# Decay attention in front of two MLPs: one group a bank for a chunk's output, and score products that alternate between heads

## The chip, the cores and the metric

The kernel runs on one core of one Trainium2 chip. The metric is the device time of one execution in microseconds (us), median of several runs.

## The reference

Decay attention over 2 batches, 8 heads, 768 tokens and 64 dimensions a head gives 1536 rows of 512. Two MLPs follow, the first gated, with 1536 hidden columns, the second with 2048:

```
intra = (q k^T * lam ** (i - j), i >= j) v
inter = (q * lam ** (i + 1)) state
state = lam ** block * state + (k * lam ** (block - 1 - j))^T v
x = intra + inter                        # all heads side by side: 1536 x 512
y = (silu(x @ w_gate) * (x @ w_val)) @ w_out
h = y @ w_in2 ;  out = (h * cos(h)) @ w_out2
```

The weights arrive as float64, all else is float32.

## The kernel before

The sequence is cut into chunks of 128 tokens: 12 chunks, six to a batch. Heads are taken in pairs; of a pair, one head's q and k, transposed, lie on partitions 0 to 63 and the other's on 64 to 127. A loop over g = 0 to 11 (here "turn g") issues, in this order and with no planner between:

- the score products of chunk g + 1 (L333: eight float32 products of 64 x 128 by 64 x 128, each run as two passes, first all four of one head of each pair into one PSUM bank, then all four of the other into a second bank), then two masking multiplications on VectorE (L338), which free the two banks;
- the transposes of q and k of chunk g + 2 (L276), copied out by ScalarE (L280, tiles qt and kt; VectorE makes qd at L284);
- in turns 6 to 11 one half of an MLP unit, twelve products (L96 to L98) on chunks that are already done;
- the state products (L309) with VectorE's addition (L320);
- the chunk's output, att_out: for each of the four pairs two score-value products (L350, 64 columns of weights, one for each half of the bank's partitions) and then, in all chunks but the first of a batch (10 of the 12), the state product of that pair (L355, 128 x 128), which adds to the same quarter of the bank. ScalarE and VectorE split the result (L90, L91: xh, xl).

Every engine takes its own instructions in that order. Loads are issued on SyncE (SP) in program order: q and k four chunks ahead, v three ahead, and in some turns one piece of weights (512 KB, tile raw, L123 and L128). The weights' float64 words are converted piecewise: `tick()` puts one VectorE step of a piece (L145, L149, L153, L158) behind a masking multiplication, a qd or a state addition. The first step of a piece also puts its absolute value on ScalarE (L143), and the last one the split (L90 on ScalarE, L91 on GpSimd). The first piece's steps stand in turn 3, where L143 comes ahead of the copies of chunk 5 on ScalarE, and L145 comes between the two maskings of chunk 4 on VectorE.

PSUM has four banks for transposes and scores (mm) and four for state, output and MLP sums (acc). Behind the attention the MLP units run with conversions between them.

Of the kernel before, what the change touches and what calls it, by code (L numbers as in the profile page):

```python
# [13 lines left out]
ALU = mybir.AluOpType  # L14
PSUM = bass.MemoryType.PSUM

# 2*pi = TWO_PI_1 + TWO_PI_2, TWO_PI_1 short so that n * TWO_PI_1 is exact in float32
TWO_PI_1 = 6.28125
TWO_PI_2 = 2.0 * math.pi - 6.28125

# [14 lines left out]
def kernel(  # L35
# [10 lines left out]
    w_out2: bass.AP,  # L46
    out: bass.AP,
):
    """Decay attention in chunks of 128 tokens, then the two MLPs with weights outermost:
    every tile of float64 weights is read once, turned into float32 on the chip and split  # L50
    there into two float32r parts of 12 significant bits each (w = wH + wL exactly); a
    product takes the passes wH xL + wL xH + wH xH."""
    nc = tc.nc
    B, H, S, D = q.shape
    P = 128
# [11 lines left out]
    CB = TB // C  # L67
    NBLK = NCH // CB

    # float64 words as pairs of int32 (low, high)  # L70
    w_gate, w_val, w_mid, w_in2, w_out2 = (w.bitcast(I32) for w in (w_gate, w_val, w_mid, w_in2, w_out2))

    const = ctx.enter_context(tc.tile_pool(name="const", bufs=1))
# [12 lines left out]
        return pool.tile([P, 512], F32, tag=where, name=where)  # L86

    def split(hi, lo, src, sub=None):
        """src = hi + lo exactly, each of 12 significant bits."""
        nc.scalar.activation(hi, src, AF.Copy)  # L90
        (sub or nc.vector).tensor_tensor(out=lo, in0=src, in1=hi.bitcast(F32), op=ALU.subtract)  # L91

    def mm3(ps, w, x, first, last):
        """ps += (wH + wL)^T (xH + xL), float32 products of 12-bit parts."""
        (wh, wl), (xh, xl) = w, x
        nc.tensor.matmul(ps, wh, xl, start=first, stop=False)  # L96
        nc.tensor.matmul(ps, wl, xh, start=False, stop=False)  # L97
        nc.tensor.matmul(ps, wh, xh, start=False, stop=last)  # L98

# [1 line left out]
    order1, order2 = [], []  # L101
    f0 = 0
    for n in GROUPS1:
# [25 lines left out]
        raw[key] = t  # L129

    def conv_steps():
        """float32 of the next piece: one vector instruction a step."""
        n = n_conv[0]
        n_conv[0] += 1
        key = pieces[n]
        words = raw.pop(key).rearrange("p (n t) -> p n t", t=2)
        lo, hi = words[:, :, 0], words[:, :, 1]
        w = cvt.tile([P, 512], I32, tag="cw", name="cw")
        t = cvt.tile([P, 512], F32, tag="ct", name="ct")
        pool = ring[n % (RING_A + RING_B) >= RING_A]  # L140
        wh = pool.tile([P, 512], F32R, tag="wh", name="wh")
        wl = pool.tile([P, 512], F32R, tag="wl", name="wl")
        nc.scalar.activation(t, hi.bitcast(F32), AF.Abs)  # L143
        # sign and top exponent bit, the low seven exponent bits and 23 of the mantissa
        nc.vector.tensor_scalar(  # L145
            out=w, in0=hi, scalar1=3, scalar2=0x3FFFFFF8, op0=ALU.logical_shift_left, op1=ALU.bitwise_and
        )
        yield
        nc.vector.scalar_tensor_tensor(  # L149
            out=w, in0=hi, scalar=-0x40000000, in1=w, op0=ALU.bitwise_and, op1=ALU.bitwise_or  # L150
        )
        yield
        nc.vector.scalar_tensor_tensor(  # L153
            out=w, in0=lo, scalar=29, in1=w, op0=ALU.logical_shift_right, op1=ALU.bitwise_or
        )
        yield
        # below float32's normal range the exponent bits left out are not the top bit's: zero there
        nc.vector.scalar_tensor_tensor(  # L158
            out=t, in0=t, scalar=2.0 ** -15, in1=w.bitcast(F32), op0=ALU.is_ge, op1=ALU.mult
        )  # L160
        split(wh, wl, t, sub=nc.gpsimd)
        wsp[key] = (wh, wl)
        yield
# [15 lines left out]
            pass  # L179
        load_piece()  # L180

# [1 line left out]
    att_stack = ExitStack()  # L183
    att = att_stack.enter_context(tc.tile_pool(name="att", bufs=2))
    qkv = {}
# [20 lines left out]
    state = [att.tile([P, NPAIR, P], F32, name=f"state{i}", bufs=1) for i in range(2)]  # L206

    def tables():
        """Powers of lam_h by doubling, falling (down[h, n] = lam_h ** (C - n), zero for n > C)
        and rising (up_p[h, n] = lam_h ** (n + 1)), and out to DRAM and back  # L210
        flip[j, h, C - 1 - i] = lam_h ** (i - j) where i >= j, else 0, and
        lrow[(h' d), pair, i] = lam_h ** (i + 1)."""
        flip = [att.tile([P, NPAIR, C], F32, tag="qd", name="qd", bufs=3) for _ in range(2)]
        anti = att.tile([P, P], F32, name="anti", bufs=1)
        nc.gpsimd.memset(anti, 0.0)
        nc.gpsimd.affine_select(
            out=anti, in_=anti, compare_op=ALU.not_equal, fill=1.0, base=1 - P, pattern=[[1, P]], channel_multiplier=1
        )
        nc.vector.memset(down[:, C + 1:], 0.0)
        nc.vector.memset(down[:, C:C + 1], 1.0)  # L220
        nc.sync.dma_start(down[:, C - 1:C], lam.rearrange("(h o) -> h o", o=1))
        n = 1
        while n < C:
            nc.vector.tensor_scalar(
                out=down[:, C - 2 * n:C - n], in0=down[:, C - n:C],
                scalar1=down[:, C - n:C - n + 1], scalar2=None, op0=ALU.mult,
            )
            n *= 2
        load_qkv(0, "qk")
        nc.sync.dma_start(down_d, down)  # L230
        nc.vector.tensor_copy(up_p[:, 0:1], down[:, C - 1:C])
        n = 1
        while n < C:
            nc.vector.tensor_scalar(
                out=up_p[:, n:2 * n], in0=up_p[:, 0:n], scalar1=up_p[:, n - 1:n], scalar2=None, op0=ALU.mult
            )
            n *= 2
        load_qkv(1, "q")
        e = down_d[:, :]
        for h2 in range(2):  # L240
            nc.sync.dma_start(
                flip[h2], bass.AP(e.tensor, e.offset + 1 + h2 * 2 * C, [[1, P], [4 * C, NPAIR], [1, C]])
            )
        nc.sync.dma_start(up_d, up_p)
        load_qkv(1, "k")
        load_qkv(0, "v")
        e = up_d[:, :]
        for h2 in range(2):
            nc.sync.dma_start(
                lrow[64 * h2:64 * h2 + 64], bass.AP(e.tensor, e.offset + h2 * C, [[0, 64], [2 * C, NPAIR], [1, C]])  # L250
            )
        return anti, flip

    def unflip(anti, flip):
        """dmask[j, h, i] = flip[i, h, C - 1 - j]: a head's flip is symmetric."""
        for h2 in range(2):
            ps = bank("acc")
            for p in range(NPAIR):
                nc.tensor.transpose(ps[:, p * C:(p + 1) * C], flip[h2][:, p, :], anti)
            nc.scalar.activation(dmask[:, h2::2, :], ps.rearrange("p (a i) -> p a i", a=NPAIR), AF.Copy)  # L260

# [1 line left out]
    xs = {}  # L263
    live = {}

# [31 lines left out]
            live[g, "kd"] = kd  # L297

    def att_state(g):
        """state(g + 1) = lam ** 128 * state(g) + k_dec^T v, block diagonal by head in a pair."""  # L300
        if g % CPB == CPB - 1:
            return
        kd, vn = live.pop((g, "kd")), qkv[g, "v"]
# [21 lines left out]
    def att_scores(g, before_mask=None, args=()):  # L325
        qt, kt = live[g, "qt"], live[g, "kt"]
        at = live[g, "at"] = att.tile([P, H, C], F32, tag="at", name="at")
        got = []
        for h2 in range(2):
            ps = bank("mm")  # L330
            r = slice(64 * h2, 64 * h2 + 64)
            for p in range(NPAIR):
                nc.tensor.matmul(ps[:, p * C:(p + 1) * C], kt[r, p, :], qt[r, p, :], start=True, stop=True)  # L333
            got.append(ps)
        if before_mask:
            before_mask(*args)
        for h2, ps in enumerate(got):
# [5 lines left out]
    def att_out(g):  # L343
        at, vn = live.pop((g, "at")), qkv[g, "v"]
        ps = bank("acc")
        inter = g % CPB != 0
        for p in range(NPAIR):
            cs = slice(p * C, (p + 1) * C)
            for h2 in range(2):
                nc.tensor.matmul(  # L350
                    ps[64 * h2:64 * h2 + 64, cs], vn[:, 2 * p + h2, :], at[:, 2 * p + h2, :],
                    start=True, stop=not inter,
                )
            if inter:
                nc.tensor.matmul(ps[:, cs], state[g % 2][:, p, :], live[g, "qd"][:, p, :], start=False, stop=True)  # L355
        xh, xl = x_tiles(g // CB)
        o = (g % CB) * C
        split(xh[:, :, o:o + C], xl[:, :, o:o + C], ps.rearrange("p (a i) -> p a i", a=NPAIR))

# [1 line left out]
    units = []  # L361
    for ph, order in enumerate((order1, order2)):
        for gi, fs in enumerate(order):
# [1 line left out]
                units += [(ph, gi, blk, f) for f in fs]  # L365
    NU = len(units)
    orders = (order1, order2)
    # the step that takes unit u's second product, and the steps a piece of weights is used in
    taken, t = [], 0
    for u in range(NU + LAG):  # L370
        while t < NU and t <= u - LAG:
# [31 lines left out]
        live[u] = (live[u], up_mm("val", f, x_tiles(blk), where))  # L403

    def produce(u):
        """The first product and the activation of unit u; what is left of it comes with finish()."""
        ph, gi, blk, f = units[u]
        if ph == 0:
            produce_gate(u)
            produce_val(u)  # L410
        else:
            up = up_mm("in2", f, x_tiles(blk, "y"))
            # cos(h) = sin(pi/2 - |h - 2 pi n|), n = round(h / 2 pi)
            n_ = tp.tile([P, TB], I32, tag="n", name="n")
            s = tp.tile([P, TB], F32, tag="s", name="s")
            nc.scalar.activation(n_, up, AF.Copy, scale=1.0 / (2.0 * math.pi))  # L416
# [55 lines left out]
                nc.sync.dma_start(out[r0:r0 + C, :], sm)  # L472

    def convert(u, due):
        """Convert what the units to come need, as slots come free and evenly over time."""
        while n_conv[0] < len(pieces):
            nxt = n_conv[0]
            if nxt >= RING and last_use[pieces[nxt - RING]] > u:
# [3 lines left out]
            conv_piece()  # L482
            due -= 1

# [1 line left out]
    with tc.manual_schedule():  # L486
        nc.vector.memset(halfpi, math.pi / 2)
        flip = tables()
# [96 lines left out]
```

## Time and profile before

| what | us |
| --- | --- |
| median of 3 runs | 646.48 (646.32 to 649.52) |
| span of the profiled execution, first to last instruction | 644.7 |
| TensorE (PE) busy in it | 631.7 (98%) |
| VectorE (DVE) busy | 455.3 (71%) |
| ScalarE (ACT) busy | 274.8 (43%) |

The page states no other time of the profiled execution than its span; the median of the runs is 1.8 us above it. Matmuls are pipelined and their ends are modelled, so TensorE's busy share says little: what a group of products occupies is read from its start to the start of the next group.

### The profile page before, as it was taken

The numbers are of one execution on the slowest core, as the hardware profiler recorded it, in microseconds if no ns is written. First come the engines' busy times: TensorE is split into PE (matmuls) and PEld (weight loads), VectorE is DVE, ScalarE is ACT, GpSimd is POOL, SyncE is SP. The second block draws the span as 40 slices with busy tenths as digits, with TensorE's granted clock in tenths as the row PEclk, the third lists the DMA queues.
The fourth block names the chain that finished last, engine by engine and source line by source line (L and its number), as shares of the span: only waits on it lengthen the run. The fifth ranks groups of instructions, "written<-read, shape, count | busy, mean of one in ns | idle before, by whom it ended". The sixth has DMA issues, their size and how long they took to land.

```text
span 644.7 us, 8244 instructions
## 1 busy us (share of the span) xinstructions
PE 631.7 (98%) x3176; PEld 517.4 (80%) x3176; DVE 455.3 (71%) x706; ACT 274.8 (43%) x464; POOL 131.3 (20%) x114
## 2 busy tenths in 40 slices
PE   6999999999999999999999999999999999999997
PEld 5778778888888878888888887788888888888885
DVE  4577746888889853388824478987797778776655
ACT  3333313555343421234313346555555555554441
POOL 1423312232332310023203244011101010100000
PEclk9999999999999999999999999999999999999999
DMA  7999312333343320034310111111111110000103
GB/s 170 219 213 225 108 34 66 104 126 111 118 131 106 127 63 1 32 99 130 99 34 15 52 57 41 35 64 37 62 41 58 36 63 2 0 1 0 67 3 128
DMA packets 66006, 49.56 MB, mean 77 GB/s; under 512 B 38816, under 2 KB 60848, under 8 KB 65968
## 3 DMA queue, kind: packets, MB, share of 16 engines
q1 hardware_dynamic: 65968, 49.04, 26.5%
q8 instruction: 25, 0.41, 0.3%
q14 instruction: 13, 0.11, 0.1%
HBM read 45.88 MB, written 3.16 MB: 76 GB/s over the span
## 4 chain that ended last, share of the span: by engine, by line
PE 73%; DVE 18%; ACT 6%; issue 1%; DMA 1%; DVEq 0%; SPq 0%; ACTq 0%
PE mm L97 11%; PE mm L96 11%; PE mm L98 11%; PE acc L96 10%; PE acc L98 10%; PE acc L97 10%; DVE cw L153 5%; DVE ct L158 3%; PE mm L333 3%; DVE cw L149 3%; PE acc L355 3%; PE acc L350 2%; PE mm L276 2%; DVE g L428 2%; DVE sum L466 2%; ACT wh L90 2%
## 5 line engine op out<-in xcount | busy, mean ns | idle before, releaser
L96 PE MATMUL mm<-xl,wh 128*128 128x512 f32 x456 | 177.5, 389 | 0.0
L97 PE MATMUL mm<-xh,wl 128*128 128x512 f32 x456 | 177.4, 389 | 0.0
L98 PE MATMUL mm<-xh,wh 128*128 128x512 f32 x456 | 177.4, 389 | 0.0
L91 POOL TENSOR_TENSOR wl<-ct,wh 128x512 fp32r<-128x512 f32 x68 | 91.4, 1345 | 390.2 <-ACT wh L90 390.2
L428 DVE TENSOR_TENSOR g<-s,mm 128x512 f32<-128x512 f32 x81 | 55.4, 683 | 65.5 <-PE mm L98 54.6
L98 PEld LDWEIGHTS mm<-xh,wh 128*128 128x128 f32 x456 | 85.6, 188 | 17.9
L96 PEld LDWEIGHTS mm<-xl,wh 128*128 128x128 f32 x456 | 85.6, 188 | 17.8
L97 PEld LDWEIGHTS mm<-xh,wl 128*128 128x128 f32 x456 | 85.6, 188 | 17.6
L90 ACT ACTIVATE wh<-ct 128x512 fp32r<-128x512 f32 x68 | 43.0, 633 | 122.9 <-DVE ct L158 122.9
L433 DVE TENSOR_TENSOR gl<-g,gh 128x512 fp32r<-128x512 f32 x84 | 58.5, 696 | 30.4 <-ACT gh L429 30.4
L96 PE MATMUL acc<-wl,gh 128*128 128x512 f32 x192 | 74.9, 390 | 1.5 <-DVE sum L464 1.1
L429 ACT ACTIVATE gh<-g 128x512 fp32r<-128x512 f32 x84 | 52.4, 624 | 53.3 <-DVE g L428 53.3
L98 PE MATMUL acc<-wh,gh 128*128 128x512 f32 x192 | 74.7, 389 | 0.0
L97 PE MATMUL acc<-wh,gl 128*128 128x512 f32 x192 | 74.7, 389 | 0.0
L153 DVE SCALAR_TENSOR_TENSOR cw<-raw,cw 128x512 int32<-128x512 int32 x68 | 67.5, 993 | 2.2
L419 ACT ACTIVATE s<-s 128x512 f32<-128x512 f32 x48 | 30.4, 633 | 72.8 <-DVE s L418 72.8
L96 PE MATMUL acc<-gl,wh 128*128 128x512 f32 x144 | 56.1, 390 | 1.5 <-DVE sum L466 1.5
L158 DVE SCALAR_TENSOR_TENSOR ct<-ct,cw 128x512 f32<-128x512 f32 x68 | 47.9, 705 | 11.7 <-ACT ct L143 6.2
L97 PE MATMUL acc<-gh,wl 128*128 128x512 f32 x144 | 56.0, 389 | 0.0
L98 PE MATMUL acc<-gh,wh 128*128 128x512 f32 x144 | 56.0, 389 | 0.0
L417 DVE SCALAR_TENSOR_TENSOR s<-n,mm 128x512 f32<-128x512 int32 x48 | 33.0, 687 | 30.7 <-ACT n L416 30.5
L149 DVE SCALAR_TENSOR_TENSOR cw<-raw,cw 128x512 int32<-128x512 int32 x68 | 49.3, 726 | 2.1
(67 smaller groups left out, 748.7 us busy)
## 6 DMA issues: line engine op xcount, KB each, us to landing
raw<-in_moe_w_out_dram SPq DMA_DIRECT2D x28, 512.0 KB, 3.2
raw<-in_moe_w_in_dram SPq DMA_DIRECT2D x16, 512.0 KB, 3.8
raw<-in_moe_w_gate_dram SPq DMA_DIRECT2D x12, 512.0 KB, 3.5
raw<-in_moe_w_val_dram SPq DMA_DIRECT2D x12, 512.0 KB, 3.6
q<-in_q_dram SPq DMA_DIRECT2D x12, 256.0 KB, 4.2
k<-in_k_dram SPq DMA_DIRECT2D x12, 256.0 KB, 4.4
v<-in_v_dram SPq DMA_DIRECT2D x12, 256.0 KB, 5.2
out_dram<-sum SPq DMA_DIRECT2D x12, 256.0 KB, 2.7
```

The lines of the kernel that those rows point to most:

```text
L90: nc.scalar.activation(hi, src, AF.Copy)
L91: (sub or nc.vector).tensor_tensor(out=lo, in0=src, in1=hi.bitcast(F32), op=ALU.subtract)
L96: nc.tensor.matmul(ps, wh, xl, start=first, stop=False)
L97: nc.tensor.matmul(ps, wl, xh, start=False, stop=False)
L98: nc.tensor.matmul(ps, wh, xh, start=False, stop=last)
L149: nc.vector.scalar_tensor_tensor(out=w, in0=hi, scalar=-0x40000000, in1=w, op0=ALU.bitwise_and, op1=ALU.bitwise_or)
L153: nc.vector.scalar_tensor_tensor(out=w, in0=lo, scalar=29, in1=w, op0=ALU.logical_shift_right, op1=ALU.bitwise_or)
L158: nc.vector.scalar_tensor_tensor(out=t, in0=t, scalar=2.0 ** -15, in1=w.bitcast(F32), op0=ALU.is_ge, op1=ALU.mult)
L417: nc.vector.scalar_tensor_tensor(out=s, in0=n_, scalar=-TWO_PI_1, in1=up, op0=ALU.mult, op1=ALU.add)
L428: nc.vector.tensor_tensor(out=g, in0=s, in1=up, op=ALU.mult)
L429: nc.scalar.activation(gh, g, AF.Copy)
L433: nc.vector.tensor_tensor(out=gl, in0=g, in1=gh.bitcast(F32), op=ALU.subtract)
```

## The change

In att_out all eight score-value products of a chunk come first and the four state products behind them. Only the first product in each half of the bank's partitions carries the start flag, and only the last one the stop flag, so the bank holds one accumulation group. In att_scores both banks are taken first, and the products go pair by pair, one head and then the other, each into its own bank. The rest of the diff strips comments and docstrings.

```
     def att_scores(g, before_mask=None, args=()):
         qt, kt = live[g, "qt"], live[g, "kt"]
         at = live[g, "at"] = att.tile([P, H, C], F32, tag="at", name="at")
-        got = []
-        for h2 in range(2):
-            ps = bank("mm")
-            r = slice(64 * h2, 64 * h2 + 64)
-            for p in range(NPAIR):
+        got = [bank("mm") for _ in range(2)]
+
+        for p in range(NPAIR):
+            for h2, ps in enumerate(got):
+                r = slice(64 * h2, 64 * h2 + 64)
                 nc.tensor.matmul(ps[:, p * C:(p + 1) * C], kt[r, p, :], qt[r, p, :], start=True, stop=True)
-            got.append(ps)
...
         inter = g % CPB != 0
+
         for p in range(NPAIR):
             cs = slice(p * C, (p + 1) * C)
             for h2 in range(2):
                 nc.tensor.matmul(
                     ps[64 * h2:64 * h2 + 64, cs], vn[:, 2 * p + h2, :], at[:, 2 * p + h2, :],
-                    start=True, stop=not inter,
+                    start=p == 0, stop=not inter and p == NPAIR - 1, skip_group_check=True,
                 )
-            if inter:
-                nc.tensor.matmul(ps[:, cs], state[g % 2][:, p, :], live[g, "qd"][:, p, :], start=False, stop=True)
+        if inter:
+            for p in range(NPAIR):
+                nc.tensor.matmul(
+                    ps[:, p * C:(p + 1) * C], state[g % 2][:, p, :], live[g, "qd"][:, p, :],
+                    start=False, stop=p == NPAIR - 1, skip_group_check=True,
+                )
```

## Rows read from the trace of the kernel before

**Rows 1.** The page: span, and busy time with shares and instructions.
```profile
span 644.7 us, 8244 instructions
...
PE 631.7 (98%) x3176; PEld 517.4 (80%) x3176; DVE 455.3 (71%) x706; ACT 274.8 (43%) x464; POOL 131.3 (20%) x114
```
**Rows 2.** Busy time by stretch, then clock, DMA share and GB/s.
```profile
20.00:27.00 7.00, 7.00 (x74) 5.42 (x71) 4.05 (x8) 1.68 (x3) 2.87 (x4) 1.00 1.07 209
27.00:33.20 6.20, 6.20 (x65) 4.74 (x65) 3.24 (x7) 1.68 (x3) 2.25 (x3) 1.00 1.15 246
...
67.50:76.60 9.10, 9.10 (x78) 6.97 (x77) 7.34 (x13) 3.88 (x7) 3.91 (x4) 1.00 0.08 27
```
**Rows 3.** Timeline of PE: start, us, line, operation, tiles, forms, count.
```profile
28.45 0.39 PE L350 MATMUL acc<-at,v 128*64 128x128 f32 x4
28.77 0.49 PE L355 MATMUL acc<-qd,state 128*128 128x128 f32 x2
29.18 0.44 PE L350 MATMUL acc<-at,v 128*64 128x128 f32 x4
...
31.55 1.71 PE L333 MATMUL mm<-qt,kt 64*128 64x128 f32 x16
33.19 0.66 PE L276 MATMUL mm<-ident,q 128*128 128x128 f32 x4
...
37.83 1.71 PE L333 MATMUL mm<-qt,kt 64*128 64x128 f32 x16
...
44.11 1.71 PE L333 MATMUL mm<-qt,kt 64*128 64x128 f32 x16
45.75 0.66 PE L276 MATMUL mm<-ident,q 128*128 128x128 f32 x4
```
**Rows 4.** Timeline of PE, turn 6, which has no state products of a chunk.
```profile
55.87 1.05 PE L350 MATMUL acc<-at,v 128*64 128x128 f32 x16
56.85 1.71 PE L333 MATMUL mm<-qt,kt 64*128 64x128 f32 x16
```
**Rows 5.** Waits from 12 to 98 us: who, for what, us, times, longest.
```profile
PEld acc L355 <- issue: 6.7, 39, 0.2
```
**Rows 6.** Score products (L333) under way in two instants: PE and PEld counts.
```profile
38.22:38.23 0.01, 0.01 (x2) 0.01 (x2) 1.00 1.19 256
38.72:38.73 0.01, 0.01 (x6) 0.01 (x3) 1.00 1.01 230
```
**Rows 7.** Timeline of ACT, turns 3 and 4.
```profile
35.47 0.68 ACT L143 ACTIVATE ct<-raw 128x512 f32<-128x512 f32 x1 [3.22 <-DMA raw<-in_moe_w_gate_dram]
...
36.53 0.59 ACT L280 ACTIVATE kt<-mm 128x512 f32<-128x512 f32 x1
...
41.33 0.60 ACT L280 ACTIVATE kt<-mm 128x512 f32<-128x512 f32 x1
```
**Rows 8.** Timeline of DVE, turns 3 and 4.
```profile
35.47 0.43 DVE L145 TENSOR_SCALAR cw<-raw 128x512 int32<-128x512 int32 x1 [1.90 <-DMA raw<-in_moe_w_gate_dram]
...
39.11 0.69 DVE L158 SCALAR_TENSOR_TENSOR ct<-ct,cw 128x512 f32<-128x512 f32 x1
40.98 0.69 DVE L91 TENSOR_TENSOR xl<-acc,xh 128x512 fp32r<-128x512 f32 x1 [1.18 <-ACT xh L90]
41.59 1.28 DVE L338 TENSOR_TENSOR at<-mm,dmask 128x512 f32<-128x512 f32 x2
```
**Rows 9.** Timeline of SP: the first piece of weights is issued.
```profile
28.98 1.06 SPq L123 DMA_DIRECT2D raw<-in_moe_w_gate_dram  x1
```
**Rows 10.** Timeline of PE: the first product behind the attention.
```profile
97.94 0.48 PE L96 MATMUL mm<-xl,wh 128*128 128x512 f32 x1
```
**Rows 11.** The chain that ended last: start, us, what.
```profile
113.19 1.41 ACT sum L462 x3
```
**Rows 12.** Timeline of PE near 227 us, idle time before in brackets.
```profile
227.52 0.50 PE L96 MATMUL acc<-gl,wh 128*128 128x512 f32 x1 [1.47 <-DVE sum L466]
```
**Rows 13.** Timeline of PE: the first score products of the run.
```profile
7.29 3.09 PE L333 MATMUL mm<-qt,kt 64*128 64x128 f32 x16 [0.69 <-ACT kt L280]
```

## The prediction

> **What bounds the kernel now.** I read the page first [rows 1]: TensorE (PE) counts as busy for 98% of the span, but that is modelled, so I went on to the busy time by stretch [rows 2], then to PE's timeline over single turns, and last to the waits. In the attention (12 to 98 us) PE's timeline is a gapless row of groups: from the start of one group to the start of the next there is nothing but its passes and some fixed cost where the form of the product changes. So there PE sets the pace, and what it saves is the kernel's, until something else is late. Two candidates for that show up. The DMA engines are full from 20 to 33 us [rows 2], and ScalarE and VectorE both wait in their order for the first piece of weights until 35.47 us [rows 7, 8]. Behind the attention, the chain that ended last leaves PE at 113.19 us, goes over ScalarE to VectorE, and returns to PE at 227.52 us, where PE waits 1.47 us [rows 11, 12].
>
> **Prices, from starts.** Two pairs of score-value passes run side by side, one in each half of the columns. Four passes take 0.32 us to the next start (28.45 to 28.77) [rows 3], sixteen take 0.98 (55.87 to 56.85) [rows 4]; the difference is six slots in 0.66, so a slot is 0.11 us and the change of form behind the group 0.10. Two state passes take 0.41 (28.77 to 29.18) [rows 3]: two slots, and 0.19 for changing into the full width and out of it. The waits confirm that this is a stall: PE's weight load sat idle before L355 39 times, 6.7 us in all, 0.17 each [rows 5].
>
> **Edit 1, one group a bank.** It removes no product and no wait for data; the eight changes of form per chunk become two. A chunk's output takes 3.10 us now (28.45 to 31.55) [rows 3]. Afterwards: sixteen score-value passes in 8 slots, 0.88, a change 0.10; eight state passes, which have the array alone, 0.88, and 0.19: 2.05. That is 1.05 us for each of the ten chunks that have state products, 10.5 in all. The two others stay as in [rows 4]. If only the change itself went and the state passes kept their 0.41 a pair, it would be 0.88 + 0.10 + 1.64 = 2.62, a saving of 0.48 a chunk; a stream of equal passes is nearer to the slots of [rows 4], so I take 1.05.
>
> **Edit 2, alternating heads.** The group takes 1.64 us now (31.55 to 33.19) [rows 3]. Less 0.19 for the changes that is 13 slots for 16 passes, so three slots already hold two passes; in one instant of the single stream two passes are under way, in one where both heads run six [rows 6]. Alternated from the start it is 8 slots and 0.19: 1.07, a saving of 0.57 a chunk, 6.8 for twelve. The bounds are no overlap at all (16 slots, 0.3 lost a chunk) and this 0.57; since the overlap of the two heads is on the trace, I take the latter. The edit moves one wait: the second product now needs the second bank, where it was the ninth.
>
> The Trainium skill, TensorEngine Tiling (Array Packing), Key Properties, says that changing the tiling mode drains the engine while changing only the tile does not. The 0.17 us before L355 agrees with the first half [rows 5]; the second half speaks for edit 2, and by it the 0.57 would stand.
>
> **Where PE's 17.3 us go.** Alone, PE would give 10.5 + 6.8 = 17.3. I follow the turns. By the scores of chunk 5 (now at 37.83 [rows 3]) three outputs and four score groups are saved: 3 x 1.05 + 4 x 0.57 = 5.4, so they could start at 32.4, or at about 33.6 if the loads of chunks 2 and 3 hold back two of the groups. But they need kt of chunk 5, which ScalarE copies behind L143, and L143 waits for the first piece of weights until 35.47; kt is done at 36.53 + 0.59 = 37.12 [rows 7]. That piece is issued at 28.98 [rows 9] behind loads that keep the DMA full from 20 us on [rows 2], so a faster PE hardly brings it forward (at most by a microsecond: what 20 to 27 us moved at 209 GB/s, 1.46 MB, takes 5.9 us at the 246 of the next stretch [rows 2]). I take none of it. So PE stands for 3.5 to 4.7 us and keeps 0.7 of the 5.4.
>
> The next turn needs 6.28 us now (37.83 to 44.11 [rows 3]), afterwards 6.28 - 0.57 - 1.05 = 4.66, so PE reaches the scores of chunk 6 at 41.8. Again it is too early. VectorE goes back to back from the same arrival: L145 at 35.47, the piece's last step at 39.11, then xl, which waits for ScalarE, then the two maskings of chunk 5 at 41.59, done at 42.87 [rows 8]. The second of them frees the second bank. Before the change only the ninth product would have waited for it; now the second does. kt of chunk 6 is done at 41.93 [rows 7], earlier. From 42.87 the group takes 1.07, so the transposes behind it start at 43.94 instead of 45.75 [rows 3]: 1.8 us saved up to there.
>
> From then on I find no wait that ends later than PE. What is left to save is six outputs (turns 5, 7, 8, 9, 10, 11) and five score groups (chunks 7 to 11): 6 x 1.05 + 5 x 0.57 = 9.15. The tightest turn is the one that now runs from 67.5 to 76.6: VectorE is busy for 7.34 of 9.10 us [rows 2], and the turn shrinks by 1.62 to 7.48, so it just fits; the DMA is busy for 0.08 of it, so loads are no longer late there.
>
> **The sum.** 1.8 + 9.15 = 10.95, so the first MLP product moves from 97.94 [rows 10] to about 87.0. What follows hangs on PE and VectorE together. The chain into the MLPs starts with a PE result at 113.19 [rows 11], so it moves as a whole, the wait at 227.52 [rows 12] with it; the loads of later pieces wait for staging that VectorE frees, and move too. The span becomes 644.7 - 10.95 = 633.8. The median of the runs is 1.8 above the profiled span and I keep that: 635.5 us.
>
> **Rivals.**
> *PE comes out of the new stall at a lower clock.* The clock column stands at 1.00 (2.4 GHz) in the stretches shown [rows 2], but the first score group took 3.09 us busy [rows 13] against 1.71 for each later one [rows 3], right after PE had begun work. If the 4.66 us of the turn behind the stall took twice as long, the scores of chunk 6 would start at 37.1 + 9.3 = 46.4 instead of 42.87: 3.5 us lost, 639.0. If full pace is back at once, nothing is lost. Against it: no row shows PE slow again later, but none shows it idle that long either.
> The Trainium skill, TensorE: Matmul & The Clock Gate, Part 1, says that an idle engine falls to half its rate until it has been busy again; by it this rival would hold, and nothing in the rows after 20 us tests it.
> *Alternation gives nothing* (PE takes the passes one after the other). Then scores cost what they do, and the wait at 42.87 still binds: 44.11 - 42.87 = 1.24, and six outputs, 6.3: 7.5 saved, 639.0. Against it: [rows 6].
> *The weights are not late*: if the first piece came five microseconds sooner, all of 17.3 would be kept, 629.2. Against it: the full DMA [rows 2].
> *No change:* VectorE becomes the pace of the late turns, because its backlog of conversion steps moves into them and its waits for later pieces and for ScalarE leave it less than the spare 0.14 us that I count. Then the late turns keep their length and only the first 1.8 us remain: about 644.7, within the 0.5% (3.2 us) that a measurement of this kernel can tell from no change.
> *Slower:* every step from one half of the rows to the other costs what a change of form does, 0.19, and the overlap ends. A score group is then 16 x 0.11 + 8 x 0.19 = 3.28, 1.64 more than now. Up to chunk 5: 4 x 1.64 - 3 x 1.05 = 3.4 late; then 7 x 1.64 - 7 x 1.05 = 4.1 more: 654. It decides from about 0.08 us a step on: (10.5 - 12 x 0.31) / 84 steps. Against it: [rows 6] again, passes of both halves run together.
>
> **How the numbers follow.** My forecast gets 0.65, with its own range of 633.5 to 637.5 (below, the microsecond of earlier weights and one for a kt or a masking that is read too late; above, a microsecond each for VectorE and for the clock). The clock gets 0.15 (up to 639), no gain from alternation 0.07 (639), weights early 0.04 (629), no change 0.05, slower 0.04. Faster by over 0.5% are the first four: 0.91. The range 630.5 to 640 holds the first three, and leaves out 0.13.
>
> **What would show it.** Right: the weight load's stalls before L355's products fall from 39 to about 10; sixteen score passes span about 1.07 us to the next group; an output with state products spans about 2.05; PE stands some 4 us before the scores of chunk 5, released by ScalarE's kt, and about 1 us before those of chunk 6, released by VectorE's masking; L143's wait for the piece grows from 3.22 us; the first MLP product comes near 87 us. Wrong: score passes that stay 13 slots; no stall near 34 us; score groups of 2 us or more after it; a shift at 87 us that is gone at 228.

## The result and the profile after

The median of four runs is 636.84 us (635.47 to 637.71), against 646.85 (646.32 to 649.52) for the kernel before, run beside it: ratio 0.9842, with a 95% interval of 0.982 to 0.9863, so 10.0 us less. The forecast was 635.5, in a range of 630.5 to 640. The profiled execution of after is its slowest run (637.71, span 635.9), so its span saves only 8.8 us [rows 1]; the point by point below goes by that span.

The page of after:
```profile
span 635.9 us, 8244 instructions
...
PE 616.8 (97%) x3176; PEld 510.9 (80%) x3176; DVE 455.0 (72%) x706; ACT 274.7 (43%) x464; POOL 131.3 (21%) x114
...
PEclk9979999999999999999999999999999999999999
```
No instruction came or went, and VectorE and ScalarE do what they did [rows 1]. PE is busy for 14.9 us less. The third slice of the clock row, 31.8 to 47.7 us, reads 7.

PE's timeline of after (start, us, line, operation, tiles, forms, count, and in brackets the idle time before):
```profile
26.48 1.04 PE L350 MATMUL acc<-at,v 128*64 128x128 f32 x16
27.46 1.16 PE L356 MATMUL acc<-qd,state 128*128 128x128 f32 x8
28.54 1.16 PE L333 MATMUL mm<-qt,kt 64*128 64x128 f32 x16
29.64 0.66 PE L276 MATMUL mm<-ident,q 128*128 128x128 f32 x4
...
37.50 2.08 PE L333 MATMUL mm<-qt,kt 64*128 64x128 f32 x16 [4.19 <-ACT kt L280]
39.51 1.12 PE L276 MATMUL mm<-ident,q 128*128 128x128 f32 x4
...
44.94 1.16 PE L333 MATMUL mm<-qt,kt 64*128 64x128 f32 x16
46.03 0.66 PE L276 MATMUL mm<-ident,q 128*128 128x128 f32 x4
...
89.17 0.48 PE L96 MATMUL mm<-xl,wh 128*128 128x512 f32 x1
...
218.76 0.50 PE L96 MATMUL acc<-gl,wh 128*128 128x512 f32 x1 [1.48 <-DVE sum L470]
```
The first four lines hold both edits: an output with state products goes from 26.48 to 28.54, 2.06 us where it took 3.10, and a score group from 28.54 to 29.64, 1.10 where it took 1.64 [rows 3]. The fifth line is the new stall: PE stands before the scores of chunk 5. The first MLP product starts at 89.17 instead of 97.94 [rows 10], 8.77 earlier, and the wait at 227.52 [rows 12] is now at 218.76, 8.76 earlier: the shift passes through the MLPs whole.

Waits of after from 12 to 90 us (who, for what, us in total, times, longest):
```profile
ACT ct L143 <- DMA raw<-in_moe_w_gate_dram: 6.6, 1, 6.6
...
PE mm L333 <- ACT kt L280: 4.9, 2, 4.2
...
PEld acc L356 <- issue: 1.2, 7, 0.2
```
The stalls of the weight load ahead of the state products went from 39 [rows 5] to 7. ScalarE's wait for the first piece of weights went from 3.22 us [rows 7] to 6.6: PE, VectorE and ScalarE come to that place earlier, and the piece does not. ScalarE's timeline of after:
```profile
35.80 0.67 ACT L143 ACTIVATE ct<-raw 128x512 f32<-128x512 f32 x1 [6.55 <-DMA raw<-in_moe_w_gate_dram]
...
36.86 0.59 ACT L280 ACTIVATE kt<-mm 128x512 f32<-128x512 f32 x1
```
The piece lands at 35.80, 0.33 us later than before, and kt of chunk 5, behind it in ScalarE's order, is done at 37.45. PE starts at 37.50.

Then comes what the forecast gave a chance but no time. The score group at 37.50 takes 2.01 us to the next start, and the turn from 37.50 to 44.94 takes 7.44 where 4.66 was forecast. Busy time by stretch of after (stretch, us, PE, PEld, DVE, ACT, POOL, granted clock, DMA share, GB/s):
```profile
34.00:35.00 1.00, 0.00 (x0) 0.00 (x0) 0.00 (x0) 0.00 (x0) 0.00 (x0) 1.00 1.21 310
...
36.00:37.00 1.00, 0.00 (x0) 0.00 (x0) 1.00 (x3) 1.00 (x3) 0.00 (x0) 0.81 1.01 188
37.00:38.00 1.00, 0.50 (x4) 0.51 (x6) 1.00 (x3) 0.44 (x1) 0.00 (x0) 0.50 0.90 179
38.00:40.00 2.00, 2.00 (x19) 1.78 (x17) 1.94 (x5) 0.00 (x0) 0.00 (x0) 0.50 1.01 219
...
43.00:44.00 1.00, 1.00 (x13) 0.83 (x10) 0.94 (x3) 0.00 (x0) 0.92 (x2) 0.77 1.05 261
44.00:46.00 2.00, 2.00 (x24) 1.78 (x24) 0.33 (x1) 0.96 (x2) 1.63 (x2) 1.00 0.25 56
```
The granted clock falls from 1.00 (2.4 GHz) towards the end of the stall, is 0.50 (1.2 GHz) when PE begins again, stays there while PE works without a gap, and is back at 1.00 by 44 us. From 34 to 35 us every engine stands, and only the DMA works.

### The profile page after: what moved, and what is told of

It is laid out like the page before. It is cut to its first block, busy times and chain, and to the rows that moved or that the text cites. A ratio compares the mean times of both kernels' runs of the same rounds, so it can differ in the third digit from the quotient of the medians.

```text
span 635.9 us, 8244 instructions
## 1 busy us (share of the span) xinstructions
PE 616.8 (97%) x3176; PEld 510.9 (80%) x3176; DVE 455.0 (72%) x706; ACT 274.7 (43%) x464; POOL 131.3 (21%) x114
## 4 chain that ended last, share of the span: by engine, by line
PE 70%; DVE 19%; ACT 6%; DMA 2%; issue 1%; SPq 1%; POOL 0%; DVEq 0%; ACTq 0%; POOLq 0%
PE mm L98 11%; PE mm L96 11%; PE mm L97 11%; PE acc L96 10%; PE acc L98 10%; PE acc L97 10%; DVE cw L153 5%; DVE ct L158 3%; DVE cw L149 3%; DVE g L432 2%; PE mm L333 2%; DVE sum L470 2%; ACT wh L90 2%; DVE cw L145 2%; PE mm L276 2%; PE acc L350 2%
```

## The experiments

Each row of the table is the median and the ratio to the kernel before, from five rounds in which the kernel before ran too (its medians there: 646.4 to 646.7).

| kernel | us | ratio, 95% interval | profiled span | us saved |
| --- | --- | --- | --- | --- |
| edit 1 alone | 638.47 | 0.9875 (0.9852 to 0.9897) | 636.4 | 8.2 |
| edit 2 alone | 641.61 | 0.9919 (0.990 to 0.9938) | 639.8 | 5.0 |
| both, the stall filled | 636.12 | 0.983 (0.9808 to 0.9852) | 634.4 | 10.5 |
| both, conversion steps later | 634.38 | 0.981 (0.9786 to 0.9834) | 632.2 | 12.3 |
| both, once more | 637.15 | 0.9841 (0.9819 to 0.9864) | 635.4 | 9.2 |
| both, steps later, one moved behind kt | 633.19 | 0.979 (0.9766 to 0.9813) | 631.1 | 13.2 |
| both, steps later and spread | 634.55 | 0.9818 (0.9806 to 0.9831) | 631.7 | 11.8 |
| both, four loads left out, zeroed at the start | 633.07 | 0.9784 (0.9761 to 0.9806) | 631.5 | 13.3 |
| before, four loads left out, zeroed at the start | 650.31 | 1.0052 (1.0035 to 1.0068) | 646.7 | -3.9 |
| both, four loads left out, zeroed in turns | 631.12 | 0.977 (0.9757 to 0.9782) | 629.3 | 15.3 |
| before, four loads left out, zeroed in turns | 646.21 | 1.0004 (0.9993 to 1.0014) | 644.1 | 0.2 |

**Edit 1 alone.** The scores go head after head again:
```diff
-        got = [bank("mm") for _ in range(2)]
-        for p in range(NPAIR):
-            for h2, ps in enumerate(got):
-                r = slice(64 * h2, 64 * h2 + 64)
+        got = []
+        for h2 in range(2):
+            ps = bank("mm")
+            r = slice(64 * h2, 64 * h2 + 64)
+            for p in range(NPAIR):
                 nc.tensor.matmul(...)
+            got.append(ps)
```


> Edit 1 without edit 2, so scores run head after head. My theory (a chunk's output falls from 3.10 to 2.05 us, ScalarE's kt of chunk 5 stays at about 37.1 to 37.5 us, and every PE gain before it is lost): PE reaches the scores of chunk 5 some 3 us early and stands; then 1.3 us are kept up to the transposes of chunk 7 and 6 x 1.05 behind it, 7.6 in all, 639; down to 5 saved if PE comes out of this stall at half its clock too. Rival (only the drains go, the state passes keep 0.41 a pair): 0.48 a chunk, 3 to 4 saved, 643.

It saved 8.2 us. PE's timeline of it:
```profile
36.68 1.71 PE L333 MATMUL mm<-qt,kt 64*128 64x128 f32 x16 [1.83 <-ACT kt L280]
41.92 1.71 PE L333 MATMUL mm<-qt,kt 64*128 64x128 f32 x16
```
The same stall stands in the same place, but 1.83 us long, and the turn behind it takes 5.24 us: 6.28 [rows 3] less the 1.04 of the output, at full pace. The mean clock of this execution is 1.00.

**Edit 2 alone.** The output's products go back to the old order, pair by pair:
```diff
-                    start=p == 0, stop=not inter and p == NPAIR - 1, skip_group_check=True,
-        if inter:
-            for p in range(NPAIR):
-                nc.tensor.matmul(..., start=False, stop=p == NPAIR - 1, skip_group_check=True)
+                    start=True, stop=not inter,
+            if inter:
+                nc.tensor.matmul(ps[:, cs], ..., start=False, stop=True)
```


> Edit 2 without edit 1, so outputs stay at 3.10 us. My theory (a score group falls from 1.64 to 1.07 us and the wait on the first piece of weights takes what is saved before chunk 5): about 0.9 kept up to the scores of chunk 6 and six groups of 0.57 behind, 4.3 saved, 642.5; the stall before chunk 5 is under 2 us and the clock stays at 1.00. Rival (alternation does little for PE, edit 1 made the change): score groups of 1.6 us and 646.5. If the two edits met no common wait, e1 and e2 together would save what both save, 10; by my theory their sum is larger than that, 11 to 12.

It saved 5.0 us. PE's timeline of it:
```profile
36.86 1.16 PE L333 MATMUL mm<-qt,kt 64*128 64x128 f32 x16 [0.61 <-ACT kt L280]
```
The group has the 1.16 us busy of the full change. So each edit gives what it should on PE, and each already runs into the wait for kt of chunk 5. The two alone save 8.2 + 5.0 = 13.2 us, together 10.0: the wait is common to both, and behind the longer stall of both together the clock is lower as well.

**The stall filled.** In front of the scores of chunk 5, four products whose result nobody uses keep PE at work:
```diff
+            if g == FILL_TURN:
+                ps = bank("acc")
+                for _ in range(FILL):
+                    nc.tensor.matmul(ps, ident, dmask[:, 0:NPAIR, :].rearrange("p a i -> p (a i)"), start=True, stop=True)
```


> The changed kernel with four products of no use (128 x 128 by 512 columns, float32) between the output of chunk 3 and the scores of chunk 5, in a bank that nobody reads: PE works through most of the stall from 33.2 to 37.5 us, and no wait is taken away. If the stall itself halves the clock and the halved clock costs 1 to 2 us, the granted clock stays at 1.00, the turn from the scores of chunk 5 to those of chunk 6 falls from 7.44 us to about 5.7 (then the masking of chunk 5 binds, near 43.2), and the kernel is 1 to 2 us faster than the changed one: about 635.2, 11 to 11.5 saved. Rival (the turn is slow for other reasons, such as its waits for VectorE and ScalarE): the turn stays near 7.4 us and the time at 636.8 or above.

PE's timeline of it:
```profile
34.11 3.60 PE L511 MATMUL acc<-dmask,ident 128*128 128x512 f32 x8
37.64 1.16 PE L334 MATMUL mm<-qt,kt 64*128 64x128 f32 x16
...
42.33 1.16 PE L334 MATMUL mm<-qt,kt 64*128 64x128 f32 x16
43.42 0.66 PE L277 MATMUL mm<-ident,q 128*128 128x128 f32 x4
...
68.84 1.16 PE L334 MATMUL mm<-qt,kt 64*128 64x128 f32 x16 [0.90 <-ACT kt L281]
```
Its busy time by stretch:
```profile
36.00:40.00 4.00, 4.00 (x36) 2.47 (x37) 3.94 (x8) 1.37 (x3) 0.00 (x0) 1.00 1.24 219
40.00:44.00 4.00, 4.00 (x61) 3.59 (x57) 2.76 (x7) 2.69 (x5) 3.00 (x4) 1.00 1.10 249
```
The start of chunk 5's scores is the same (37.64), but the clock is 1.00 and the turn takes 4.69 us instead of 7.44: the lower clock cost 2.75 us in its place. I had expected a turn of about 5.7, with the masking of chunk 5 as its limit. The transposes start at 43.42, 2.6 earlier than in after. Of that, the span keeps 1.5 and the medians 0.7 to 1.0, with intervals that overlap: part is paid back before the scores of chunk 10 (68.84), where PE waits 0.90 us for kt, a wait that after does not have. VectorE's timeline of the same kernel answers another question:
```profile
41.83 1.28 DVE L338 TENSOR_TENSOR at<-mm,dmask 128x512 f32<-128x512 f32 x2
```
The two maskings of chunk 5 end at 43.11, and the scores of chunk 6 had started at 42.33. They do not wait for the masking, and neither PE nor its weight load has a wait for it at the transposes behind them (43.42).

**Conversion steps later.** No step of the conversion is issued before turn 4's state products, so L143 no longer stands ahead of kt of chunk 5:
```diff
+    hold = [True]
...
+            if hold[0]:
+                return
...
+            if g == CONV_TURN:
+                hold[0] = False
```


> The changed kernel with the conversion steps held back until the state products of turn 4, so that neither ScalarE nor VectorE waits in turn 3 for a piece that lands at 35.8 us; every load stays where it is. My theory (the wait for the first piece ate 5 of PE's gain and the clock 1 to 2 more): no stall before the scores of chunk 5, the clock at 1.00, nearly all of 17.3 saved, 629.5 to 631. Rival (the loads of q and k or VectorE's backlog set the pace as soon as this wait is gone): a new wait of PE in turns 5 to 8, and 634 or more.

It saved 12.3 us and missed what I expected of it; the new wait that the rival named is there. PE's timeline of it:
```profile
32.94 1.16 PE L337 MATMUL mm<-qt,kt 64*128 64x128 f32 x16
...
43.86 1.16 PE L337 MATMUL mm<-qt,kt 64*128 64x128 f32 x16 [1.93 <-ACT kt L284]
```
The stall before chunk 5 is gone. But before chunk 7 PE now waits 1.93 us. ScalarE's timeline shows for what:
```profile
39.48 0.60 ACT L284 ACTIVATE qt<-mm 128x512 f32<-128x512 f32 x1 [1.14 <-PE mm L280]
42.69 0.63 ACT L91 ACTIVATE wh<-ct 128x512 fp32r<-128x512 f32 x1 [2.61 <-DVE ct L159]
43.23 0.58 ACT L284 ACTIVATE kt<-mm 128x512 f32<-128x512 f32 x1
```
The split of the first piece, which waits for VectorE's last step, now stands between the copies of qt and kt. It is the same fault in another place: a conversion instruction that waits, ahead of a copy that PE needs.

**One step moved behind kt.** The step that was issued behind qd goes behind the copy of kt:
```diff
+            if nm == "kt" and g % CPB:
+                tick()
...
-                tick()
```


> The changed kernel with the conversion steps held back as before (from the state products of turn 4 on), and the step that stands behind a qd moved behind the copy of kt, so that the split of a piece on ScalarE no longer stands between qt and kt. With steps held back PE stood 1.93 us before the scores of chunk 7 for a kt behind such a split. If that order is the cause, this wait goes and 1 to 2 us more are saved than the 12.3 of holding back alone: 632.5 to 633.5. If the conversions themselves are late (the first MLP half needs them), the wait moves to its products and the time stays at 634.

PE's timeline of it:
```profile
37.61 1.16 PE L338 MATMUL mm<-qt,kt 64*128 64x128 f32 x16
41.84 1.16 PE L338 MATMUL mm<-qt,kt 64*128 64x128 f32 x16
```
and its waits from 12 to 90 us:
```profile
PE acc L98 <- POOL wl L92: 2.0, 3, 0.9
```
The wait before chunk 7 is gone. With 633.19 us this is the fastest kernel of the study that computes all of the reference: 13.2 us saved where the change saves 10, and 0.9 more than without this move, with intervals that overlap. What is left is PE's wait for the low part of the weights, since pieces are converted later.

**Steps spread.** To mend that too, the first piece's steps go from turn 4's second masking to turn 5's, the second piece's from turn 6 on:
```diff
-            if hold[0]:
+            if turn[0] < CONV_TURN or not converting and n_conv[0] == 1 and turn[0] < 6:
                 return
...
-            tick()
+            if not (turn[0] == CONV_TURN and h2 == 0):
+                tick()
```


> The changed kernel, the whole computation, with the first piece's steps from the second masking of turn 4 to the second masking of turn 5, the second piece's from turn 6 on, and the step behind a qd moved behind the copy of kt. In e8 PE waited 0.9 us for the split of each of the first pieces and 0.7 us for a kt. If the first piece is ready earlier, the first of these waits goes: 632.3 to 632.9, at most 1 us under e8's 633.2. If VectorE as a whole is the limit of turns 6 to 10, it is no faster than e8.

It took 634.55 us and did not beat the one before; the intervals overlap. PE's timeline of it, before the scores of chunk 7:
```profile
43.23 1.16 PE L338 MATMUL mm<-qt,kt 64*128 64x128 f32 x16 [1.22 <-ACT kt L284]
```
PE waits 1.22 us for kt again, and 1.4 for the low part. Which order of steps is best was not settled.

**The change once more**, run beside the next two kernels.

> The changed kernel once more, beside the others of this call. If its slow turn behind the stall is a matter of the clock, spans go with the granted clock: about 635 us at 0.993 and 633.7 at 0.997, a median of 636 to 637.

PE waits 4.1 us in one piece, the turn behind it takes 7.23 us (37.22 to 44.45), the MLPs start at 88.68. Over the nine runs of the change, these five and the first four, the time goes with the mean granted clock: 635.5 to 636.0 us at 0.997, 636.8 to 638.0 at 0.993 to 0.995.

**Four loads left out.** Two kernels, the change and the kernel before, don't load the first four pieces of weights (2 MB); their tiles are zeroed on GpSimd, so those weights are zeros, while each conversion runs as ever:
```diff
+        if n_loaded[0] <= NOLOAD:
+            raw[key] = zeros[n_loaded[0] - 1]
+            return
...
+        zeros = [stg.tile([P, 1024], I32, tag="raw", name="raw") for _ in range(NOLOAD)]
+        for t in zeros:
+            nc.gpsimd.memset(t, 0)
```


> The changed kernel without the loads of the first four pieces of weights (2 MB): the tiles are zeroed by GpSimd at the start, so those weights are zeros, and every conversion step stays where it is. Theory A (the late landing of weights is what takes PE's gain): the stall before the scores of chunk 5 goes, the clock stays at 1.00, and all of 17.3 is saved but a microsecond for the tight turn 8: 629.5 to 630.5. Theory B (the order on ScalarE and VectorE, which put conversion steps ahead of kt and of the maskings, takes it even if the data is there): new waits for kt in turns 5 to 8 and 632 to 634.

> The kernel before, with the same four loads left out (those weights are zeros). In it PE stands nowhere for these pieces, so by both theories nothing is gained: within 1 us of 646.7, though VectorE and ScalarE lose waits of 1.9 and 3.2 us. If it gains several microseconds, the weights were late already before the change and the account is wrong.

The second of them should have stayed at the time of the kernel before, and took 3.9 us more. PE's timeline of the change in this form:
```profile
12.67 1.61 PE L263 MATMUL acc<-anti,qd 128*128 128x128 f32 x6 [3.27 <-DMA qd<-down_d]
```
PE waits 3.27 us for the decay tables. Their first steps run on VectorE while GpSimd zeroes:
```profile
1.76 3.63 POOL L500 MEMSET raw<- 128x1024 int32 x4
2.09 4.62 DVE L228 TENSOR_SCALAR down<-down 8x1 f32<-8x1 f32 x7 [1.07 <-DMA down<-in_lam_dram]
```
These seven steps take 4.62 us, where after takes 1.76. In the kernel before without the loads they take 4.63, and PE waits 1.77 us for the tables. So I moved the zeroing, one tile a turn in turns 0 to 3:
```diff
-        zeros = [...]
-        for t in zeros: ...
+            if g < NOLOAD:
+                zeros.append(stg.tile([P, 1024], I32, tag="raw", name="raw"))
+                nc.gpsimd.memset(zeros[g], 0)
```


> The changed kernel, again without the loads of the first four pieces of weights (those weights are zeros), but with the zeroing put into turns 0 to 3, one tile a turn on GpSimd, so that it no longer stands beside the tables at the start, which came 3 us late with it. Theory A (the late landing takes PE's gain): no stall before the scores of chunk 5, clock at 1.00, first MLP product about 82.5 to 83, 629.5 to 630.5. Theory B (the order of steps on ScalarE and VectorE takes it): waits for kt in turns 5 to 8 and 632 or more.

> The kernel before, without the same four loads and with the same zeroing in turns 0 to 3. PE stood for none of them: 645.5 to 647. Beside e9 it gives what the change is worth where the weights are not late: by the sum of PE's groups 17.3, less what the loads of chunks 2 and 3 hold back, 15.5 to 17.3; by theory B 14 or less.

Now the kernel before is where it was (646.21, ratio 1.0004): the late loads cost it nothing. The change takes 631.12, between the ranges of the two theories. VectorE's seven steps take 1.76 us again. PE's timeline of the change:
```profile
33.05 1.16 PE L338 MATMUL mm<-qt,kt 64*128 64x128 f32 x16
...
64.22 1.16 PE L338 MATMUL mm<-qt,kt 64*128 64x128 f32 x16 [0.92 <-ACT kt L285]
```
and its busy time where after stood still:
```profile
33.00:37.00 4.00, 4.00 (x61) 3.50 (x60) 2.75 (x6) 2.09 (x4) 1.58 (x2) 1.00 1.06 226
```
No stall before chunk 5 and no lower clock, as theory A has it; but PE waits for kt before the scores of chunk 10. Between these two kernels the change is worth 15.1 us by medians and 14.8 by spans, under the 15.5 to 17.3 expected by the sum of PE's groups and over theory B's 14. With the real loads it is worth 10.0, and 9.2 when run once more: the late weights take five to six.

## Why the prediction was right, and where its steps failed

**Edit 1, right.** Forecast 2.05 us for an output with state products, measured 2.06, so 1.04 saved for each of ten. The equal state passes run one a slot.

**Edit 2, right.** Forecast 1.07, measured 1.10. Edit 2 alone shows the same group with the other edit undone, so the overlap comes from the alternation. The Trainium skill's sentence on tiling modes, weighed in the prediction (TensorEngine Tiling (Array Packing), Key Properties), agrees with that: the sixteen passes change only their tile, and measure 1.10 us, where a change of form at every step between the two halves was the price of the slower rival, 3.28.

**PE alone gives 17.3, about right.** With the measured groups it is 10 x 1.04 + 12 x 0.54 = 16.9. Where the weights are not late, the spans show 14.8. In that pair the scores of chunk 2 start no earlier than in the kernel before (18.96 against 18.77), because PE waits for the loads of q and k ahead of them. So two of the twelve groups give nothing, as the prediction allowed, and 10.4 + 5.4 = 15.8 is left, of which 0.92 goes in the wait for kt before the scores of chunk 10.

**The stall before the scores of chunk 5, right in place, cause and size.** Forecast start 37.12, PE idle for 3.5 to 4.7; measured 37.50 and 4.2. The later start is the piece's landing, 0.33 later. That the weights are the cause is shown from both sides: with the loads left out, and with L143 issued later, the stall is gone.

**"The second of them frees the second bank", wrong.** The step let the scores of chunk 6 wait for VectorE's masking until 42.87. With the stall filled they start at 42.33 while the masking runs to 43.11. So their products do not go into the two banks under masking. Without this wait PE would have reached them at 37.12 + 4.66 = 41.8, with kt of chunk 6 done at 41.93 [rows 7].

**The clock at nothing, wrong.** The forecast took full pace behind the stall. The rival that did not had 0.15 and lost 3.5 us; measured, it cost 2.75 to 2.8 in its place. Among the signs of being wrong stood "score groups of 2 us or more after it", and the group at 37.50 takes 2.01. The Trainium skill, TensorE: Matmul & The Clock Gate, Part 1, which stood beside the rival, agrees with the row: 0.50 after 4.2 us without work.

**The sum.** The two failed steps have opposite signs. The scores of chunk 6 started at 44.94, 2.07 after the forecast: 0.38 for the later kt, 2.78 for the clock (7.44 - 4.66), less 1.09 for the masking that was not waited for (42.87 - 41.78). So up to the transposes nothing was saved (46.03 against 45.75 [rows 3], 0.28 lost) where 1.8 was forecast. From there to the MLPs 9.05 was saved (52.19 before, 43.14 after) where 9.15 was forecast. The two make 8.77, the span's 8.8. The profiled execution is the slowest of the four; the median saved 10.0 against 10.95. That it came so near is partly luck: the wait that did not come paid for 1.09 us of the clock that the sum had left out.

**The tightest turn "just fits", true of after, but not of a faster PE.** The turn of the scores of chunk 10 takes 7.44 us in after, from the scores of chunk 9 on, against 7.48 forecast, with no wait in it. As soon as PE comes to it earlier, with the stall filled or the loads left out, it waits 0.90 or 0.92 us for kt. ScalarE's timeline with the loads left out and zeroed in turns:
```profile
61.99 0.63 ACT L91 ACTIVATE wh<-ct 128x512 fp32r<-128x512 f32 x1 [1.96 <-DVE ct L162]
...
63.59 0.58 ACT L285 ACTIVATE kt<-mm 128x512 f32<-128x512 f32 x1
```
A split that waits for VectorE's last step stands ahead of the copy here too. The spare 0.14 us was read from busy times, and these say nothing of the order in which ScalarE and VectorE come to a copy.

**The MLPs carry the shift, right.** 8.77 at their start, 8.76 at the wait that was at 227.52.

## What to carry to other kernels

Group passes of one form, and let passes that use different rows of the array alternate: both are worth what the slots in the trace of before say. Then look for what comes next in the in-order queues of the other engines: here a conversion that waits for a load stood ahead of the copy that PE needed, and took five to six of fifteen microseconds, of which issuing it later, with one step moved behind the copy, gave back three to four. Where a forecast makes PE stand for several microseconds, price the turn behind it at the lower clock too.

## What the runs showed of the hardware that was not expected

The granted clock was 0.50 after PE had stood for 4.2 us, and stayed there for about six more microseconds in which PE had work the whole time. With stalls of 1.83 us (edit 1 alone) and 1.93 (conversion steps later) the mean clock of the profiled execution was 1.00.

A long stall is not the only place of a lower clock. Other executions of these two kernels, of which there is no trace, had a mean of 0.993 and 0.996 (edit 1 alone, 640.92 and 639.23 us) and 0.997 (steps later, 636.3). And in the trace with the stall filled the clock is low near the start (columns as above):
```profile
16.00:19.00 3.00, 2.88 (x24) 2.18 (x26) 1.31 (x3) 1.20 (x2) 0.00 (x0) 0.50 1.33 219
```
Ahead of it PE had waited only 0.69 and 1.20 us. With the loads left out and zeroed in turns it waited 0.79 and 1.18 us in the same place, and the clock stayed at 1.00. It cost the filled run 0.27 us at most (kt of chunk 5 done at 37.37, its scores at 37.64). Why the clock fell there stays open.

In the first 13 us of after the column reads 1.00, and yet the first score group is busy for 2.08 us, as long as the one at clock 0.50 (37.50):
```profile
7.29 2.08 PE L333 MATMUL mm<-qt,kt 64*128 64x128 f32 x16 [0.69 <-ACT kt L280]
```
The column alone does not show a slow start.
